# Last stores dealt over three queues, six pieces for the first batch's last chunk, and 140 half-size sets instead of 141

## The chip, the cores and the metric

The kernel runs on one core of one Trainium2 chip. The metric is the time of one execution in microseconds on the device; lower is better. The engines are named as in the profile: PE (TensorE, matrix products), ACT (ScalarE), DVE (VectorE), POOL (GpSimd) and SP (SyncE, which here only starts DMAs). DMAs are started from SP and ACT (hardware queues) and from POOL (a software queue).

## The reference

Inputs: `q`, `k`, `v` of shape 4 x 6080 x 256 (fp32), a scalar `tau` = 1, `w_in` of 256 x 2048 and `w_out` of 2048 x 256. Output: 24320 x 256 fp32.

```python
qn = q / (np.linalg.norm(q, axis=1, keepdims=True) + 1e-06)     # norm over the 6080 tokens
kn = k / (np.linalg.norm(k, axis=1, keepdims=True) + 1e-06)
s = kn.transpose(0, 2, 1) @ qn / tau                            # 256 x 256 for each batch
a = softmax(s)                                                  # over the last axis
x = (v @ a).reshape(24320, 256)
h = x @ w_in
g = 0.5 * h * (1 + tanh(sqrt(2 / pi) * (h + 0.044715 * h**3)))
out = g @ w_out
```

## The kernel before, in words

**Opening.** For batch 0 the 256 x 256 matrix kᵀq ("gram") and the sums of squares of q and k over the tokens ("ss") must be complete before anything else can start. q and k come in chunks of token rows (128 tokens to a row of the tile), cast to bf16 by POOL's DMAs. The last chunk, eight rows each of q and k, comes in pieces, `PIECES` (L137): (which, first row, end row), with which = 0 for q and 1 for k. DVE and ACT square the rows (`square_rows`), PE does the gram rows (`gram_first`, L210) and the sums (`ss_rows`, L229 and L235). Then come the scores, the softmax, and `aw` = a @ w_in, the attention matrix folded into the first weights, so that the rest is an MLP on v.

**Main part.** The 24320 tokens are cut into 25 blocks, numbered m = 0 to 24, each of two halves of up to 512 tokens. Batches 0 to 2 have six blocks each (5 x 1024 tokens and 960), batch 3 has seven (5 x 1024, 704 and 256). So block 22 has 1024 tokens, 23 has 704 and 24 (`LAST`) has 256. The hidden width 2048 is 16 chunks of 128, numbered 0 to f in hexadecimal. The first product of a block is done in one of two ways:

- plainly: a token `m:jct` is chunk c on half t (2 matmuls, L586; t = 2 means both halves at once), `m:Jct` its gelu on ACT (L598);
- as a half-size set, `m:sp...`, for the pair of chunks 2p and 2p+1 on both halves: seven half-size products m1 to m7 on sums of weights (`sw`, tokens `b:w..`, DVE) and sums of v (`tv`, tokens `m:vs..`, DVE) in place of eight, with two copies on ACT (`cq`, L669, and `y5`, L672), two additions on DVE (`ap`, L674, and `ax`, L677) and four gelus on ACT (`G0`, `G1`, `Gr`, `Gx`).

The second product of a block is seven products `M1` to `M7`, each in two parts A and B (L765), of sums `T..` and `x1` made by DVE, and is put together by `y5`, `y6`, `ap`, `ax`, `a12`. `c11`, `c12`, `c21`, `c22` turn the result (L794, DVE) into output layout, and `m:O0` and `m:O1` store the two halves, each by `store` (L808) in four DMAs, bi = 0 to 3. In block 22 one such DMA has 128 KB, in block 23 88 KB, in block 24 32 KB.

**What sets the order.** `ORDER` (L990) is one long table of tokens, written out by hand or by a planner; the program issues the work in exactly this order, and each engine does its part of it in this order. Other tokens are loads (`lq`, `lk`, `lv` on POOL; `lt`, the transposed copy of v, on SP), the work on the next batch's gram, and `b0:aw..`/`b0:ac..` (the later parts of `aw`: product and scaling). PSUM is eight banks: each product takes the bank that came free longest ago (`take`), and gives it back (`give`) when its reader is done. So a change of order also changes which product waits for which reader.

**Semaphores of the DMAs.** The DMAs of SP and ACT share eight completion semaphores, dealt in turn, and POOL's DMAs have another eight. A DMA is issued only after the last DMA with the same semaphore has landed. At the end (L1320) SP waits for all sixteen, in the order of their numbers.

Of the kernel before, what the change touches and what calls it, by code (L numbers as in the profile page):

```python
# [18 lines left out]
def kernel(  # L19
# [777 lines left out]
    def store(m, tj):  # L797
        b, t0, hc = SB[m]
        r0 = b * N + t0 + tj * hc
        dst = out[r0 : r0 + hc, :].rearrange("(x t) (b c) -> b t x c", t=32, b=4)  # L800
        ot = OT.pop((m, tj))
        for bi in range(4):
            eng = nc.sync
            if m == LAST:
# [3 lines left out]
            eng.dma_start(out=dst[bi], in_=ot[bi * 32 : bi * 32 + 32, 0 : hc // 32].rearrange("p x h c -> p x (h c)"))  # L808
# [187 lines left out]
0:j51 0:J21 0:jb1 0:s7m6 0:ja1 0:Jb1 0:s6ap 0:J51 0:J91 :pF0 0:Ja1 1:j00 0:s7ap :pS3 b0:w02 1:lt1
1:J00 0:s6m3 0:s7m3 0:s6m7 1:j50 0:s6ax 1:J50 0:j01 0:s7G1 b1:r0.0 :pS1 :pF1 0:jb0 0:j61 0:j11
0:s6G1 b1:r0.1 1:j10 0:Jb0 b1:lq1 0:s7m7 b1:lk1 b1:lq2 0:s6Gx 0:s7ax 0:s6m4 0:M1A 0:J01 1:j30 4:lv0
0:s7m4 0:J11 b1:r0.2 0:M1B b1:lq3 :pA12 0:T3a 0:s6Gr 0:s7Gx 1:J10 b1:lk3 :pS2 b1:lk2 b1:r0.3 0:x1
1:j31 1:j21 0:s7Gr 0:J61 1:vs0 0:M2A 3:lv0 1:j41 1:J30 1:J31 1:s3m1 1:j01 0:T1a 1:J21 2:lv1 0:M2B  # L1000
0:T2a 1:J41 0:T3b 1:s3cq 1:j11 b1:dk0 b1:lk4 1:J01 0:c11 b1:r1.0 b0:w03 b1:r1.1 b1:zk1 1:s3m2 0:T1b
1:J11 0:M5A b1:r1.2 0:M6A 1:s3m5 1:s4m1 1:s4m5 1:vs1 1:s3G0 b1:r1.3 0:T2b b1:zq0 1:s3m6 1:s3y5 0:M5B
1:s4cq 1:s4y5 1:s4m6 8:lv0 b1:lq4 1:s4m2 0:y5 1:s3ap 1:s4ap :pS4 0:M6B 1:s4G0 1:s4m3 0:ap 1:s3m7
1:j51 1:s3ax 1:s3m3 :pNA b1:r2.0 1:s4m7 b1:zq1 1:vs2 b1:r2.1 b1:lq5 1:J51 b1:f1.1 1:s3Gx 0:M7A
1:s3G1 1:s5m1 1:s3m4 1:s4G1 1:s5cq 1:s3Gr b1:r2.2 1:s4ax 0:T4a 0:M3A b1:lk5 1:s5m5 1:s5y5 b1:r2.3
1:s5m2 2:lv0 b1:f0.1 1:s4Gx 1:s5m6 0:M3B 1:s5ap 1:s5G0 1:s4m4 b1:zq2 1:s6m1 b1:r3.0 1:s6m5 1:s5m7
1:s5m3 0:M7B 0:c12 1:s6cq b1:f1.2 1:s5ax 1:s6m6 1:s6y5 1:s5m4 1:s6m2 1:s5G1 b1:r3.1 1:s5Gr b1:r3.2
2:lt0 1:s4Gr 1:j20 0:T4b 1:s6ap 0:ax 1:j40 1:s6m3 b1:dk2 1:s5Gx 1:s6G0 b1:r3.3 0:c22 1:T3a 1:s7m1
1:s6m7 1:J20 1:s7cq 0:M4A 1:s7m5 1:J40 1:s6ax 0:M4B 1:s7y5 1:s7m6 b1:r4.0 0:c21 1:s6G1 1:s7ap b1:zk3
1:s6Gx b1:zq3 1:M1A 1:T1a 1:M1B 1:s7m7 b1:r4.1 1:s7m3 0:O1 b1:r4.2 1:s6m4 1:x1 1:s7G1 2:lt1 1:s7ax  # L1010
2:j20 1:s7m4 1:s7Gx 1:s7Gr 1:T2a 1:s7m2 1:s6Gr 2:j10 1:s7G0 1:M2A 2:s2m1 1:T3b 2:j30 b1:f3.1 1:T1b
1:M6A 2:J10 2:vs0 1:M2B 2:J20 b1:zq5 b1:lq6 1:c11 b1:lk6 2:s2cq 2:vs1 1:M5A 2:s2m5 b1:zk5 2:s2m2
1:T2b 2:j11 2:s2y5 b1:lq7 2:s2m6 1:M5B 2:s2G0 2:s2ap 2:j01 1:T4a 2:s2m3 2:J11 2:J30 1:y5 2:s3m1
1:M6B 3:lv1 b1:f1.3 2:s2G1 2:s3cq 2:s2m7 1:ap b1:f2.1 2:J01 2:vs2 2:s3m5 2:s3m2 2:s3y5 2:s3m6 2:s2ax
2:s4m1 1:M3A 1:M3B 2:s3G0 b1:zq4 2:s4cq 2:s3ap 1:c12 b1:r4.3 2:s2Gx 2:s2m4 2:s3m3 2:s4m2 2:s4m6
1:T4b 2:s3m7 2:s2Gr 2:s3ax 2:s4G0 2:s4m5 2:s4y5 2:s3G1 2:j21 1:M7A 3:lt0 0:O0 b1:r5.0 2:J21 2:s4ap
2:s5m5 2:s3m4 2:s4m7 2:s5m1 b1:dk4 1:M7B 2:s3Gx 2:s6m5 2:s4m3 b1:r5.1 2:s3Gr 2:s5y5 b1:f3.2 2:s4ax
2:s5cq 2:s6y5 1:ax 2:s4m4 2:s4G1 1:c22 2:s5m6 2:s5ap 1:M4A 2:s5m2 2:j31 2:s4Gx 2:s5m7 1:O1 b1:f3.3
b1:f5.1 2:s4Gr 2:s6m1 2:s5m3 2:s5ax 3:lt1 2:s5G0 2:J31 2:s6cq 1:M4B 2:s5m4 b1:r5.2 2:s6m6 2:s7m1
b1:r5.3 b1:f3.4 1:c21 2:s5Gx 2:s5G1 b1:r6.0 2:s7m5 2:s5Gr 2:s7cq 2:s6m2 2:s6ap 2:s6m3 2:s6m7 2:s7m6  # L1020
2:s7m2 2:s7y5 2:s6G0 2:T3a 2:j00 2:s6G1 2:s7ap 3:j00 2:s6ax b1:lk7 b1:r6.1 b1:f4.1 b1:lq8 b1:zq6
3:j30 2:J00 2:s6Gx b1:dk6 2:s7G0 b1:r6.2 b1:r6.3 b1:lk8 2:s7m7 2:T1a 2:s7m3 2:M1A 2:s7G1 2:s7ax
b1:f5.2 2:s6m4 2:M1B b1:lk9 3:j31 2:s7m4 3:j11 3:J30 2:T2a 2:s6Gr 2:s7Gx 4:lv1 3:J31 b1:f6.1 b1:lq11
2:s7Gr 3:j20 3:vs0 2:M5A 3:s2m1 b1:lq9 2:T3b 3:J11 2:x1 3:J00 3:j21 b1:zq7 3:vs1 2:M2A 3:j01 3:J20
2:M2B b1:f5.3 2:T1b 3:J21 2:c11 3:s2cq 5:lv1 b1:r7.0 b1:zk7 3:s2m5 3:s2y5 2:T2b b1:r7.1 2:M6A 3:J01
b1:r7.2 3:s2m2 3:s2m6 3:s2ap b1:r7.3 5:lv0 3:vs2 3:s3m1 2:M5B b1:lk10 b1:zq8 3:s2G0 3:s2m3 3:s2m7
2:M6B 3:s3cq 2:y5 b1:f5.4 b1:lq10 3:s3m5 3:s3m6 3:s2ax b1:f7.1 2:ap b1:r8.0 3:s2G1 3:s3m2 3:s3y5
3:s2m4 3:j10 3:s2Gx b1:lk11 3:s3G0 2:M3A b1:f7.2 3:s4m1 b1:dk8 3:J10 b1:r8.1 3:s2Gr 3:s3ap b1:f8.1
2:M3B 3:s4cq 3:s3m7 3:s4m5 b1:f7.3 3:s3m3 3:s4m2 3:s4m6 2:c12 b1:zk9 3:s4y5 3:s5m1 2:M7A b1:r8.2
3:s4G0 3:s3G1 3:s5m5 3:s3ax 3:s4ap 3:s3Gx 3:s5cq 3:s4m7 b1:r8.3 3:s3m4 3:s4m3 b1:r9.0 3:s5y5 2:T4a  # L1030
b1:r9.1 4:lt1 3:s4ax 3:s3Gr 3:s5m6 3:s5m2 b1:r9.2 2:T4b 3:s4G1 3:s5G0 2:M7B 3:s5ap 2:ax b1:r9.3
3:s4Gx b1:zq9 3:s6m5 3:s5m7 3:s6m1 b1:r10.0 b1:f7.4 b1:r10.1 3:s6cq 2:M4A 4:lt0 3:s5ax 3:s5m3 3:s4m4
3:s6y5 b1:r10.2 3:s5Gx 3:s5G1 3:s4Gr 3:s6m6 3:s5m4 3:s6m2 b1:r10.3 b1:f9.1 3:s6G0 b1:dk10 3:s6ap
3:T3a b1:r11.0 3:s7m1 3:s5Gr 3:s7m5 3:s6m7 3:s6ax 3:s7cq b1:f9.2 3:s6m3 2:M4B 3:s7m6 3:s7m2 3:s7y5
3:s6G1 5:lt0 3:s6Gx b1:r11.1 3:s6m4 4:j21 1:O0 b1:r11.2 3:s7G0 3:s7ap 4:J21 2:c21 3:s7m7 3:s7ax
3:s7m3 4:j01 4:j11 3:s7m4 3:s6Gr 3:s7G1 3:T1a b1:r11.3 4:j00 4:s2m1 4:s3m1 3:s7Gx 4:vs0 3:T3b 2:O0
b1:gc 5:lt1 3:s7Gr 4:J11 3:M1A 3:M1B 4:s3cq 4:J00 3:M5A 4:vs1 4:s3m2 3:T1b 4:s2cq 4:s2m2 4:J01 3:x1
4:s3m6 4:s2m5 4:s3G0 3:T2a 3:M5B 4:vs2 4:s2m6 4:s3m5 4:s2y5 b1:zq10 3:M6A 3:T2b 4:s3y5 3:y5 7:lv0
3:M6B 3:M2A 4:s2ap 4:s2G0 4:s3ap 4:s2m7 b1:zq11 b1:f9.3 4:j31 3:ap 4:s3m3 b2:lq0 b1:zk11 4:s2ax
4:s3G1 3:M2B b1:f9.4 3:T4b 4:J31 b1:f11.1 4:s2m4 4:s2Gx 4:s3m7 4:s3ax b2:lk0 4:s2m3 4:s2Gr 4:j20  # L1040
b1:f10.1 8:lv1 4:s2G1 4:s4m5 3:M3A 4:s4m1 4:J20 6:lv0 4:s4cq 3:M3B 4:s4y5 3:c11 4:s3m4 4:s3Gr b2:lk2
6:lv1 4:s4m2 4:s4G0 4:j30 4:s5m5 4:s4m6 3:c12 b1:f11.2 4:s5m1 4:s3Gx b2:lq2 3:M7A 4:s4ap 4:s4m3
4:s5cq 2:c22 4:J30 4:s4G1 4:s4m7 4:s6m1 4:s5m6 4:s5y5 4:s5m2 3:M7B b1:f11.3 4:s6cq 4:s4ax 4:s4m4
b1:f11.4 b1:ss 4:s5ap 4:s5G0 3:T4a 4:s5m3 4:s6m5 4:s4Gx 4:s4Gr 4:s5m7 4:s5G1 4:s6m6 b1:sv 5:j11
b1:pow 4:s6m2 4:s6y5 4:j10 4:s5ax 4:s5m4 5:j21 5:J11 3:ax 4:s6ap 3:c22 4:s7m1 b1:kf 6:lt1 3:M4A
4:s5Gx 4:s5Gr 4:J10 4:s6m3 2:O1 4:s6m7 4:s7m5 5:J21 3:M4B b1:kr 4:s6G0 4:s7cq 4:s6G1 b1:krp 4:M1A
4:T3a 3:O1 5:j41 4:s7m6 4:s7y5 4:s6ax b1:S0 b1:S1 4:s7m2 3:c21 4:s7ap 4:M1B 4:s7m7 5:j50 4:T1a
b1:th1 5:j31 4:s6Gx 4:s6m4 b1:th0 4:s7G0 5:J41 b1:dn 4:x1 5:j30 4:s7m3 4:s7ax 4:s7m4 4:s6Gr 5:J31
4:s7G1 6:lt0 4:M2A 5:j51 4:s7Gr 5:J50 5:j01 5:j20 5:J30 4:T2a b1:rc0 5:j10 5:J01 5:vs0 5:j40 5:J51
# [275 lines left out]
```

## Time and profile before

| | us |
|---|---|
| time before, median of 3 runs | 682.67 (682.46 to 682.88) |
| the profiled execution's own time | 682.53 |
| its span, first to last instruction | 680.7 |
| PE busy | 659.0 |
| ACT busy | 639.9 |
| DVE busy | 631.3 |
| POOL busy | 89.4 |
| mean granted TensorE clock | 0.998 |

The profile is of one execution. Times in its views are counted from the span's start. A matmul's row gives its duration from entering to leaving, and consecutive matmuls overlap; the spacing of their starts is what they cost. A row of the chain of waits gives a start, a length, and the work that held the end of the kernel back in that time. In brackets behind a row of the timeline stands the idle time of the engine before it, and what ended it. A row of a DMA's issuing gives the time that the queue spent on starting it; its flight ("to landing") comes after.

### The profile page before, as it was taken

The page shows a single profiled execution, that of the slowest core. Times are in us where ns is not written, and L with a number is a line of the kernel's source. Part 1 is how long each engine was busy: PE and PEld are TensorE (multiplying, and loading weights), DVE is VectorE, ACT ScalarE, POOL GpSimd, SP SyncE. Part 2 cuts the span into 40 slices and gives each one's busy share as a digit, 9 for nine tenths or more (in the row PEclk, how much of TensorE's full clock was granted, in tenths as well). Part 3 has the DMA queues.
Part 4 walks back from the last instruction along what each step waited for, and adds up shares of the span by engine and source line. Part 5 has one row for each costly group of instructions (what it writes and reads, how often), then busy time and mean ns, then how long its engine had stood idle before and what let it go on. Part 6 is the DMA issues. An engine that isn't in the chain of part 4 may idle for free.

```text
span 680.7 us, 10235 instructions
## 1 busy us (share of the span) xinstructions
PE 659.0 (97%) x3415; PEld 332.1 (49%) x3475; DVE 631.3 (93%) x934; ACT 639.9 (94%) x1241; POOL 89.4 (13%) x163
## 2 busy tenths in 40 slices
...
GB/s 242 208 256 140 133 106 172 116 122 169 90 109 88 132 180 110 103 107 107 139 140 78 88 128 137 86 142 136 49 79 63 63 86 117 47 92 36 69 44 121
DMA packets 164773, 78.80 MB, mean 116 GB/s; under 512 B 148608, under 2 KB 153152, under 8 KB 164000
## 3 DMA queue, kind: packets, MB, share of 16 engines
...
## 4 chain that ended last, share of the span: by engine, by line
PE 88%; DMA 4%; ACT 4%; DVE 1%; issue 1%; POOL 0%; SPq 0%; DVEq 0%; ACTq 0%; POOLq 0%
PE u L765 23%; PE rb L654 17%; PE j L586 12%; PE p L765 11%; PE qb L654 8%; PE c L765 5%; PE G L308 4%; DMA qk<-in_k_dram 4%; PE qa L654 4%; PE awp L527 2%; ACT g L598 1%; ACT qa L669 1%; ACT g L682 0%; ACT yw L672 0%; ACT sq L278 0%
## 5 line engine op out<-in xcount | busy, mean ns | idle before, releaser
L765 PEld LDWEIGHTS <-wcomb 128*128 128x128 bf16 x1400 | 134.7, 98 | 145.4 <-issue 0.7
L765 PE MATMUL u<-t,wcomb 128*128 128x512 bf16 (+3 forms) x588 | 144.2, 368 | 0.5
L598 ACT ACTIVATE g<-j 128x512 bf16<-128x512 f32 (+2 forms) x204 | 123.2, 657 | 1.6 <-PE j L586 1.5
L586 PE MATMUL j<-vT,aw 128*128 128x512 bf16 (+3 forms) x425 | 114.8, 367 | 0.7 <-DVE aw L419 0.3
L674 DVE TENSOR_TENSOR qb<-rb,yw 128x512 f32<-128x512 f32 (+2 forms) x141 | 95.9, 682 | 7.2 <-ACT yw L672 3.0
L677 DVE TENSOR_TENSOR xw<-rb,yw 128x512 f32<-128x512 f32 (+2 forms) x141 | 94.6, 672 | 6.7 <-PE rb L654 4.5
L654 PE MATMUL rb<-tv,sw 128*128 128x512 bf16 (+2 forms) x275 | 100.3, 374 | 0.4
L765 PE MATMUL p<-g,wcomb 128*128 128x512 bf16 (+3 forms) x385 | 95.3, 368 | 0.8
L688 ACT ACTIVATE g<-xw 128x512 bf16<-128x512 f32 (+2 forms) x141 | 94.5, 673 | 0.4 <-DVE xw L677 0.3
L672 ACT ACTIVATE yw<-qb 128x512 f32<-128x512 f32 (+2 forms) x141 | 89.2, 639 | 1.4 <-PE qb L654 0.9
L669 ACT ACTIVATE qa<-rb 128x512 f32<-128x512 f32 (+2 forms) x141 | 89.8, 641 | 0.8 <-PE rb L654 0.2
L682 ACT ACTIVATE g<-qb 128x512 bf16<-128x512 f32 (+2 forms) x141 | 88.2, 636 | 1.9 <-PE qb L654 1.7
L685 ACT ACTIVATE g<-rb 128x512 bf16<-128x512 f32 (+2 forms) x141 | 88.5, 639 | 0.3
L679 ACT ACTIVATE g<-qa 128x512 bf16<-128x512 f32 (+2 forms) x141 | 88.6, 637 | 0.2
L654 PEld LDWEIGHTS <-sw 128*128 128x128 bf16 x564 | 55.2, 98 | 58.0 <-DVE ot L794 0.4
L586 PEld LDWEIGHTS <-aw 128*128 128x128 bf16 x440 | 42.7, 98 | 43.3 <-issue 1.7
L654 PEld LDWEIGHTS <-aw 128*128 128x128 bf16 x423 | 41.4, 98 | 42.5 <-DVE aw L540 0.2
L746 DVE TENSOR_TENSOR t<-g,g 128x2048 bf16<-128x2048 bf16 (+3 forms) x50 | 58.2, 1164 | 0.9 <-ACT g L595 0.4
L738 DVE TENSOR_TENSOR g<-g 128x2048 bf16<-128x2048 bf16 (+3 forms) x50 | 58.2, 1163 | 0.2
L744 DVE TENSOR_TENSOR t<-g,g 128x2048 bf16<-128x2048 bf16 (+3 forms) x50 | 58.1, 1162 | 0.2
L748 DVE TENSOR_TENSOR t<-t,g 128x2048 bf16<-128x2048 bf16 (+3 forms) x50 | 57.6, 1157 | 0.0
L321 POOL DMA_DIRECT2D vb<-in_v_dram x47 | 24.1, 514 | 240.4 <-PE rb L654 103.3
...
## 6 DMA issues: line engine op xcount, KB each, us to landing
...
wst<-in_moe_w_out_dram POOLq DMA_DIRECT2D x2, 1024.0 KB, 11.3
...
```

The lines of the kernel that those rows point to most:

```text
L586: GATE[0] = nc.tensor.matmul(hp[:, :n].rearrange("p (t x) -> p t x", t=2) if t == 2 else hp[:, :n], lhsT=AW[b][:, cc, fc * 128 : fc * 128 ...
L598: nc.scalar.activation(g[:, t, fc % 8, :hc], hp[:, :hc], AF.Gelu_apprx_tanh)
L654: GATE[0] = nc.tensor.matmul(acc[:, :hc], lhsT=lhs, rhs=rhs, start=i in (1, 5), stop=True, skip_group_check=True)
L669: nc.scalar.activation(Q0[m, p][:, :hc], RB[m, p][:, :hc], AF.Copy)
L672: nc.scalar.activation(YW[m, p][:, :hc], Q1[m, p][:, :hc], AF.Copy)
L674: nc.vector.tensor_add(Q1[m, p][:, :hc], RB[m, p][:, :hc], YW[m, p][:, :hc])
L677: nc.vector.tensor_add(XW[m, p][:, :hc], RB[m, p][:, :hc], YW.pop((m, p))[:, :hc])
L679: nc.scalar.activation(g[:, 0, e, :hc], Q0.pop((m, p))[:, :hc], AF.Gelu_apprx_tanh)
L682: nc.scalar.activation(g[:, 1, e, :hc], Q1.pop((m, p))[:, :hc], AF.Gelu_apprx_tanh)
L685: nc.scalar.activation(g[:, 0, e + 1, :hc], RB.pop((m, p))[:, :hc], AF.Gelu_apprx_tanh)
L688: nc.scalar.activation(g[:, 1, e + 1, :hc], XW.pop((m, p))[:, :hc], AF.Gelu_apprx_tanh)
L765: GATE[0] = nc.tensor.matmul(ACCS[m, acc][:, :hc], lhsT=wcomb[:, w, fc, :], rhs=x[:, fc, :], start=first and k_ == 0, stop=k_ == 3, skip_g ...
```

## The change

There are three parts.

1. The last chunk of batch 0 comes in six pieces in place of five: q rows 0-3, k rows 0-2, k 3-4, k 5-7, q 4-6, q 7. The squares, gram rows and sums that follow are cut and ordered to match.
2. The four stores of 23:O0 go to SP, POOL, ACT and SP; all four of 23:O1 go to POOL; the last two of 22:O0 and 22:O1 go to POOL. (Before: of block 23 the first two of each half to SP, the last two to POOL; of block 22 all to SP.) Those of block 24 stay with ACT and SP by turns.
3. The table has 4054 tokens in place of 4061. The set 0:s6 (15 tokens) is taken out, and its chunks c and d of block 0 are done plainly (8 tokens: jc0, jc1, jd0, jd1 and their gelus). The tokens of blocks 0 to 3 ahead of 3:s6m1 and those after 23:s4ax stand in another order; from 3:s6m1 to 23:s4ax the two tables are the same.

```diff
-    PIECES = [(0, 0, 4), (1, 0, 5), (1, 5, 8), (0, 4, 6), (0, 6, 8)]
+    PIECES = [(0, 0, 4), (1, 0, 3), (1, 3, 5), (1, 5, 8), (0, 4, 7), (0, 7, 8)]
...
             if m == LAST:
                 eng = (nc.scalar, nc.sync)[bi % 2]
-            elif m == LAST - 1 and bi > 1:
+            elif m == LAST - 1 and tj == 0:
+                eng = (nc.sync, nc.gpsimd, nc.scalar, nc.sync)[bi]
+            elif m == LAST - 1 or m == LAST - 2 and bi > 1:
                 eng = nc.gpsimd
...
-        for i in range(4):
+        for i in range(3):
             gram_first(c, i)
         ss_rows(c, 0, range(0, 4))
+        gram_first(c, 3)
         ss_rows(c, 1, (0, 1, 4))
         square_rows(c, 1, 5, 8, "dve")
-        square_rows(c, 0, 4, 6, "dve")
+        square_rows(c, 0, 4, 7, "dve")
         ss_rows(c, 1, range(5, 8))
-        for i in (4, 5):
+        for i in (4, 5, 6):
             gram_first(c, i)
-        ss_rows(c, 0, range(4, 6))
-        square_rows(c, 0, 6, 8, "dve")
-        for i in (6, 7):
-            gram_first(c, i)
-        ss_rows(c, 0, range(6, 8))
+        ss_rows(c, 0, range(4, 7))
+        square_rows(c, 0, 7, 8, "dve")
+        gram_first(c, 7)
+        ss_rows(c, 0, range(7, 8))
...
 ORDER = """                       # the first tokens
-0:j00 0:J00 0:j10 0:j20 b0:aw2 0:J20 b0:aw3 0:j30 b0:aw5 b0:aw4 b1:lq0 0:J30 b0:ac2 0:J10 b0:ac3
-b0:aw6 b0:aw7 b0:ac5 0:j60 b0:ac4 b0:ac6 b0:w00 b0:w01 0:j50 0:J60 0:j70 0:s6m1 1:lv1 0:J70 0:vp1
...
+0:j00 0:j10 b0:aw3 b0:aw2 0:j20 b0:ac2 b0:ac3 0:j30 0:J30 b0:aw5 b0:ac5 b0:aw4 b0:ac4 b0:aw7 b0:aw6
+0:J20 0:j50 0:J00 b0:w00 b0:ac7 0:J10 b0:ac6 0:j60 0:vp1 0:j40 b1:lq2 0:vc10 0:j90 0:vc11 0:J50 0:jc0
+0:s7m1 b1:lq0 0:J60 0:J40 1:lv1 0:vs0 b1:lk0 0:J90 0:Jc0 0:jd0 0:vs1 0:ja0 0:j01 0:Jd0 0:jb0 0:s7cq
...
                                # the last tokens
-23:c21 24:T4b 24:y5 23:M2B 24:y6 24:M3A 24:M7A 24:T4a 24:M7B 23:c11
-24:ax 24:M3B 24:a12 24:M2A 23:O1 24:M2B 24:c22 24:M4A 23:O0 24:c12 24:M4B 24:c21 24:O1 24:c11 24:O0
+24:y5 24:M6B 24:T4a 24:y6 23:O1 23:M2B 24:M3A 23:c21 24:M7A 24:M7B 24:T4b 24:M3B 23:c11
+23:O0 24:M2A 24:ax 24:M2B 24:a12 24:M4A 24:c22 24:c12 24:c11 24:M4B 24:c21 24:O1 24:O0
```

More of the change, by code (lines that the diff above doesn't have):

```diff
@@ L996 @@
[L996 to L1049, printed above, removed]
@@ L1056 @@
-5:s6cq 4:M7A 5:s5m7 5:s4Gx b2:dk0 5:s6m5 5:s4m4 5:s6m6 5:s6y5 5:s5ax 5:s6m2 5:s5m3 4:M7B 5:s4Gr
-5:s6ap 6:j40 5:s5m4 b1:w02 4:ax 5:s6G0 5:s5G1 5:s6m7 b1:w10 5:s5Gx 5:s7m1 5:s7m5 4:M4A 5:s5Gr 5:s6ax
-7:lt0 5:s7cq 5:s7y5 5:s7m6 4:c22 5:s6m3 b1:w01 5:s7ap 4:M4B 4:c21 6:j50 6:J40 5:s7m2 5:s6Gx 5:s6m4
-5:s7m7 b2:zk1 6:j01 6:j21 5:s7G0 5:s7m3 b1:w12 b1:w03 6:s3m1 5:s7ax 5:T3a 5:s6Gr 6:J50 5:s7m4 4:O0
-6:J01 5:M1A 5:M1B 3:O0 7:lt1 5:s7Gr 6:vs0 6:s3cq 5:s6G1 6:j10 6:j11 5:s7G1 5:x1 6:s3m2 b1:w11 6:vs1
@@ L1124 @@
-11:s2y5 11:s2G0 10:M5B 11:s3y5 11:s2ap 11:s3m1 11:J00 11:s2m7 11:s2m3 b2:w00 11:s2ax 10:M6A 11:s2m4
-11:s3cq 11:s2G1 11:s3m6 10:y5 11:s2Gr 11:s3m2 10:T4a 11:s3G0 11:s3ap 11:s4m1 10:M6B 11:j20 16:lv0
-11:s4m5 b2:w01 11:s3m3 11:s4cq 16:lv1 11:s3m7 11:s2Gx 10:ap 11:s4m2 10:M3A b2:w10 11:J20 11:s3ax
-11:s3m4 11:s4y5 11:s3G1 11:s4m6 11:s4ap 14:lv1 10:M7A b3:lq0 11:s3Gx 11:s3Gr 11:s5m5 11:s4G0 11:s5m1
-11:s4m7 11:s5y5 11:s6m1 11:s5cq 10:T4b b3:lk3 11:s4m3 10:M3B 11:s4ax 11:s4m4 b2:w12 11:s5m6 b3:lq3
@@ L1204 @@
-16:M5A 17:s2G1 b3:w02 17:s3cq 15:O0 17:s3y5 17:s2m7 b3:aw7 17:s3m6 17:s3m2 17:s2G0 b3:ac7 17:s2ax
-b3:w00 17:s3G0 16:M5B 16:y5 17:s3ap 16:T4a 17:s5m1 17:s4m1 17:s4cq 17:s2m4 16:M6B 17:s3m3 17:s4m6
-b3:w10 16:ap 17:s3m7 17:s2Gr 17:s3G1 17:s2Gx 17:s4m2 17:j00 17:s4m5 b3:w11 17:s4G0 16:M7A 17:s4y5
-17:s5cq 17:s3ax 16:M7B 17:s5m6 17:J00 17:s3m4 17:s4ap 15:O1 17:s5m5 17:s4m7 17:s3Gx b3:w01 16:ax
-19:lv1 17:s4m3 16:M3A 17:s5y5 17:s4ax 17:s5ap 17:s3Gr 17:s5m2 17:s4G1 b3:w03 17:s6m1 19:lt1 17:s4m4
-17:s4Gx 17:s5m7 17:s5ax 17:s6cq 16:T4b 17:s5m3 16:M3B 17:s5G1 17:s4Gr 17:s6m6 17:s5Gx 17:s5m4
@@ new lines @@
+0:M1B 0:T3a b1:r0.0 0:J51 0:x1 0:j71 b1:r0.1 b1:lk2 0:s7G1 b1:lq1 0:s7Gr 0:J71 b1:lk1 b1:r0.2 0:Jc1
+8:lv0 1:s3m1 b1:r0.3 1:j31 1:j20 :pS2 0:M2A 1:J30 :pS1 3:lv0 0:M2B 1:vs0 1:J31 1:s3cq 1:s3m2 1:J20
+0:s7Gx 1:j11 1:s3G0 0:T1a b1:lk5 0:T2a 1:vs1 1:j51 2:lv1 1:j41 0:T3b 1:J11 1:s3m6 0:c11 1:j21 0:M6A
+b1:lk3 0:T1b :pNA 1:J51 1:j01 1:s3m5 b1:zq0 1:J41 0:M5A 0:M5B b1:lq4 1:J01 1:j00 b0:w03 1:s3y5 0:T2b
+1:s4m1 1:s3ap 1:J21 b1:r1.0 1:s4m5 0:y5 b1:r1.1 :pS4 b1:r1.2 1:vs2 1:J00 1:s3m7 0:M6B 1:s3ax 1:s3m3
@@ new lines @@
+5:s6m7 b1:w10 5:s5Gx 5:s7m1 5:s7m5 4:M4A 5:s5Gr 5:s6ax 7:lt0 5:s7cq 5:s7y5 5:s7m6 4:c22 5:s6m3
+b1:w01 5:s7ap 4:M4B 4:c21 6:j50 6:J40 5:s7m2 5:s6Gx 5:s6m4 5:s7m7 b2:zk1 6:j01 6:j21 5:s7G0 5:s7m3
+b1:w12 b1:w03 6:s3m1 5:s7ax 5:T3a 5:s6Gr 6:J50 5:s7m4 4:O0 6:J01 5:M1A 5:M1B 3:O0 7:lt1 5:s7Gr 6:vs0
+6:s3cq 5:s6G1 6:j10 6:j11 5:s7G1 5:x1 6:s3m2 b1:w11 6:vs1 6:j41 5:s7Gx 6:J10 5:T1a 5:M2A 6:s3m5
+5:M2B 6:s3m6 5:T3b 6:J11 b2:zq1 6:vs2 5:T1b 6:s3y5 6:J21 6:s3ap 5:T2a 5:M5A 6:J41 5:M5B 6:s3G0 6:j20
+6:s3m3 6:j30 b1:w13 b2:zq0 5:T2b 6:s3m7 6:s4m1 8:lt1 6:s3ax 5:M6A 5:y5 6:J20 5:M6B 6:J30 6:s3m4
@@ new lines @@
+7:s7y5 b2:r5.0 8:J01 7:s6ax 7:s7m2 b2:lk8 7:s6G1 b2:r5.1 b2:f4.1 7:s5m4 13:lv1 7:s7G0 7:s7m6 7:s6Gx
+8:j10 8:J10 7:s6m4 8:j20 7:s7ap b2:r5.2 7:s5Gr 7:s7m7 8:J20 7:T3a 8:j11 9:lv1 7:s7ax 8:J11 7:s7Gx
+7:T1a 7:s7m3 7:M1A 7:s7m4 8:s2m1 b2:r5.3 8:vs0 7:s7G1 7:s7Gr 8:s2cq 7:s6Gr 8:vs1 8:j00 b2:r6.0 7:M1B
+7:T3b 8:s2m5 7:T2a 8:j30 8:s2m6 8:s2y5 8:J00 8:s2m2 8:s2ap 8:J30 b2:r6.1 8:j21 b2:r6.2 7:M5A 8:s2m3
+8:vs2 b2:r6.3 7:T1b 7:x1 8:s2G0 8:s2m7 8:s3m1 8:s2ax 8:s2G1 7:M2A 7:M2B 8:s2m4 8:J21 7:T2b b2:zk7
@@ new lines @@
+b2:r11.2 9:s5ap b2:f9.4 8:ax 9:s4G1 10:J20 b2:r11.3 9:s5m3 9:s7m1 9:s4Gr 9:s5m7 9:s6m5 9:s4Gx 9:j00
+b2:f10.1 b2:gc 8:M4A 9:s5G1 9:s6cq 9:s6y5 9:J00 10:lt1 9:s5ax 9:s6m6 b2:f11.2 9:s7cq 9:s6m2 b2:f11.3
+9:s6ap 9:s5m4 8:M4B 9:s7m5 9:s6m7 9:s5Gr 9:s5Gx 9:s7m6 9:s7m2 9:j30 b2:f11.4 9:s7y5 8:c21 9:s7G0
+9:s6ax 9:s6G0 9:s6m3 10:j30 b2:ss 9:s7ap 9:s6m4 10:j10 7:O1 8:c22 9:J30 13:lt1 9:s7m7 10:s2m1 b2:sv
+9:T3a 9:s6Gx 9:s7m3 9:s7ax 9:T1a 10:s3m1 9:s6Gr 9:M1A 9:s7m4 10:J30 10:vs0 9:s6G1 10:s2cq 9:s7G1
```

501 lines of the change are left out of this document (276 added, 225 removed).

## The prediction

> **What bounds the kernel now.** The page first: which engine is full, and what the chain of work that ended last is made of.
>
> ```profile
> PE 659.0 (97%) x3415; PEld 332.1 (49%) x3475; DVE 631.3 (93%) x934; ACT 639.9 (94%) x1241; POOL 89.4 (13%) x163
> PE 88%; DMA 4%; ACT 4%; DVE 1%; issue 1%; POOL 0%; SPq 0%; DVEq 0%; ACTq 0%; POOLq 0%
> ```
>
> Matmuls make the time: 88% of the chain. An average hides the stages, so the table by stretches comes next (per engine busy us and instruction count; then clock, DMA share, GB/s).
>
> ```profile
> 37.30:60.00 22.70, 22.07 (x115) 10.68 (x117) 20.09 (x38) 21.13 (x42) 4.74 (x8) 1.00 0.84 191
> 60.00:100.00 40.00, 39.79 (x198) 19.56 (x201) 39.41 (x54) 40.00 (x73) 7.40 (x15) 1.00 0.82 143
> 674.40:680.70 6.30, 0.00 (x0) 0.00 (x0) 0.52 (x2) 0.00 (x0) 0.31 (x1) 0.82 0.48 92
> ```
>
> From 60 to 100 us PE is busy 39.79 of 40, and ACT 40.00: both full, so ACT too can set the pace there. In the first 23 us after the opening both have holes. The last 6.30 us hold no matmul at all: only stores. So three places can move: the opening (before 37.3), the holes up to 60 us, and the 6.3 us of stores. The order table is unchanged from token 3:s6m1 to 23:s4ax; I take the middle as rigid and only carry a shift through it. The profiled execution took 682.53 us, 680.7 of it span and 1.83 around it; it lies 0.14 under the median 682.67, so I add my sum to the median. About 0.2% of this, 1.37 us, is what a measurement of this kernel can tell from no change.
>
> **Part 1, six pieces.** The chain of waits at the end of the opening (start, us, what):
>
> ```profile
> 31.42 1.03 PE G L210 x8
> 32.63 0.87 PE ss L235 x6
> 34.48 0.09 PE ss L229 x4
> 34.59 0.27 ACT lnq L378
> ```
>
> After the k piece that lands at 31.4, the chain holds matmuls without a gap: it is PE's backlog, not data. The last data, a two-row q piece, is squared on DVE at:
>
> ```profile
> 33.68 0.43 DVE L182 TENSOR_TENSOR sq<-qk 128x512 bf16<-128x512 bf16 x1 [0.28 <-DMA qk<-in_q_dram]
> DMA packets 2032, 1.82 MB, mean 202 GB/s; under 512 B 140, under 2 KB 1778, under 8 KB 2032
> ```
>
> The second row is the DMA view of 27 to 36 us. One row of the chunk is 128x256 bf16, 65.5 KB; at 202 GB/s it takes 0.32 us. So the three-row piece q4-6 lands about one row before the end of the data, 33.66-0.32 = 33.34, and the last row near 33.7. DVE squares three rows in at most 0.56 (a 768-wide square at 31.40 took that), 33.34 to 33.9, and the last one by 34.2. PE meanwhile has six matmuls of rows 4 to 6 to do (0.11 each, from 1.03 for eight less the overhang) and reaches the last sum near 34.4, as before. What hides the sixth piece is this backlog; without it, the piece's own fixed cost (0.1 at most; I have no row for it) shows. Term: +0.05, between -0.1 and +0.2. All later GpSimd loads move by one semaphore; the first of them, a weight load of the 1.2 MB that follow, is wanted only after 35 us: no cost.
>
> **Part 2, one half-size set fewer, blocks 0 to 3 in a new order.** The set's 7 matmuls become 8: one 512-wide one more. ACT's 6 operations become 4, DVE's 2 go. Prices by start-to-start spacing, since row durations overlap:
>
> ```profile
> 49.62 1.46 PE L586 MATMUL j<-vT,aw 128*128 128x512 bf16 x6
> 43.61 0.59 PE L586 MATMUL j<-vT,aw 128*128 128x512 bf16 x2
> 44.56 0.38 PE L654 MATMUL qa<-vT,aw 128*128 128x512 bf16 x1 [0.35 <-DVE sw L620]
> 50.92 0.38 PE L654 MATMUL rb<-tv,sw 128*128 128x512 bf16 x1
> 51.43 1.08 PE L586 MATMUL j<-vT,aw 128*128 128x512 bf16 x4
> 37.33 1.28 ACT L421 ACT_TABLE_LOAD   x1
> 38.62 1.09 ACT L598 ACTIVATE g<-j 128x512 bf16<-128x512 f32 x2
> 42.07 0.60 ACT L598 ACTIVATE g<-j 128x512 bf16<-128x512 f32 x1 [1.07 <-PE j L586]
> ```
>
> Six in 1.46 with the last 0.38 long: (1.46-0.38)/5 = 0.216 a matmul. Two ACT operations span 1.09, one 0.60: 0.49 each. So PE pays +0.216 and ACT is relieved of 2 x 0.49 = 0.98.
>
> The holes: the second of the two at 43.61 starts at 43.83; the next matmul should follow 0.216 later, at 44.04, and starts at 44.56: 0.52 lost to the weight sums on DVE (L620). From 50.92 to 51.43 is 0.51, so 0.30 lost. Four matmuls in 1.08 against 3 x 0.216 + 0.38 = 1.03: 0.05. These three are 0.87 of what PE loses before 60 us; smaller stalls, each near the last one, bring my walk of the trace to 1.1 (an estimate).
>
> The new order puts the set's matmuls behind more plain ones, so its weight sums (tokens b0:w10, w01, w11) have longer to be ready; walking it by the spacings above, with PSUM's eight banks taken and given in the table's order, I find two stalls left, about 0.25 (1:s3m1 wants the bank of 0:s7G1) and 0.08: 0.33. The price of this order: ACT's first gelu is now J30, the fourth chunk, after eight matmuls of j and four of aw: 37.34 + 12 x 0.216 + 0.16 of overhang = 40.1 rather than 38.62. ACT starts 1.5 later but then finds four chunks ready; before, it idled 1.07 at 41.0 and in smaller pieces around it, and it has 0.98 less to do. So ACT should reach 60 us no later than before. Its cover is those holes of before; if they reappear, its 40.00 of 40.00 carries any lateness on. Net for PE: +0.22 - (1.1-0.33) = -0.55; bounds -0.85 (no stall left) and +0.2 (all as before).
>
> One load is moved on a queue that matters: block 1's second v load now issues behind two q loads on GpSimd, not one.
>
> ```profile
> 43.41 0.53 POOL L321 DMA_DIRECT2D vb<-in_v_dram  x1 [2.68 <-PE rb L654]
> DMA to landing us min/median/max: 7.5/7.5/7.5
> L333 SPq DMA_TRANSPOSE vT<-vb x1: 1335/1335/1335, 52.5 to 52.5; - x1
> DMA to landing us min/median/max: 3.1/3.1/3.1
> 59.27 1.08 PE L586 MATMUL j<-vT,aw 128*128 128x512 bf16 x4
> ```
>
> Before, it landed at 50.9, its transposed copy issued at 52.5 and landed at 55.6, and the first matmul on it ran at 59.27. One 256 KB load more ahead of it is 1.3 us at 202 GB/s: 52.2, still before the copy's old time. The 3.6 us to its use cover it.
>
> **Part 3, the stores.** Here a wait does go. All HW stores (SP and ACT) share eight completion semaphores dealt in a ring; a store first waits until the ring's previous user has landed. GpSimd has eight of its own.
>
> ```profile
> 674.35 4.17 SPq L808 DMA_DIRECT2D out_dram<-ot  x4
> 674.36 2.09 ACTq L808 DMA_DIRECT2D out_dram<-ot  x4
> DMA to landing us min/median/max: 3.3/3.3/3.3
> 674.65 0.28 DVE L794 STREAM_TRANSPOSE ot<-c 128x128 f32<-128x128 f32 x1
> SPq L808 <- DMA out_dram<-ot: 2.5, 1, 2.5
> L808 SPq DMA_DIRECT2D out_dram<-ot x2: 315/369/423, 677.7 to 678.1; - x2
> DMA to landing us min/median/max: 1.5/1.5/1.6
> L1320 SPq EVENT_SEMAPHORE  x4: 17/28/28, 678.6 to 678.8; - x4
> ```
>
> The data is ready at 674.93 (the transpose at 674.65), yet SP's last two stores issue at 677.7 and 678.1: 2.5 us on a DMA, ACT's store of the same block's other half (issued 674.36; the 3.3 is its flight, so it landed near 677.7). They land 1.5 and 1.6 after, the last at 679.7; from there to the span's end is 1.0.
>
> After, by the rings of the two compiled programs, the last four stores find block 23's 88 KB stores ahead of them: SP's first waits for ACT's, ACT's second and SP's second for SP's two. By the neighbours:
>
> ```profile
> L808 SPq DMA_DIRECT2D out_dram<-ot x2: 316/390/465, 673.2 to 673.6; - x2
> DMA to landing us min/median/max: 1.9/2.1/2.4
> 675.30:676.50 1.20, 0.00 (x0) 0.00 (x0) 0.00 (x0) 0.00 (x0) 0.00 (x0) 1.00 0.98 200
> 677.70:678.50 0.80, 0.00 (x0) 0.00 (x0) 0.00 (x0) 0.00 (x0) 0.00 (x0) 0.92 0.00 0
> L808 POOL DMA_DIRECT2D out_dram<-ot x4: 627/642/688, 667.8 to 674.1; - x4
> out_dram<-ot SPq DMA_DIRECT2D x4, 32.0 KB, 1.9
> out_dram<-ot ACTq DMA_DIRECT2D x4, 32.0 KB, 2.9
> ```
>
> ACT's stores fly 1.0 longer than SP's (2.9 against 1.9). SP's 88 KB ones take up to 2.4, so ACT's, issued near 673.4, lands 673.4 + 2.4 + 1.0 = 676.8 at worst, 675.9 at best (1.9 in place of 2.4, issued 673.3 less what the queue saves); I take 676.3. Then SP issues at 676.3 and 676.7 instead of 677.7 and 678.1, 1.4 sooner. But the DMA engines are 0.98 busy until the queue empties near 677.9, so the flight is not 1.5 but towards 1.9: landing 678.6, between 678.3 and 679.3, against 679.7: -1.1.
>
> Given back: SP ends by waiting for each semaphore in number order, (678.8-678.6)/3 = 0.07 apart. Before, the last store was on number 6 of 0 to 7, one wait before the end; after, it is on number 1, with six behind: five more x 0.07 = +0.35. GpSimd's five stores take at most 0.69 each to write, and four of them belong to 23:O1, which stands ahead of 23:O0 in the table: off the path. PE's tail is reordered with the same matmuls; I walk +0.05 there. Sum of part 3: -1.1 + 0.35 + 0.05 = -0.7; bounds -1.1 (six waits free) and 0 (flights stretch until the queue is as late as it was).
>
> A rule that speaks against this part: the Trainium skill, "DMA: Bandwidth & Descriptors", section "Issuing engines are not separate DMA queues", says that DMAs from scalar, sync and gpsimd run on the same 16 engines, and that starting them on several saves only the time to start them. The 0.98 at 675.3 agrees; the 0.00 from 677.7 to 678.5 does not: there the engines stand idle while a store waits for a semaphore. By the rule part 3 would be worth nothing, as SP starts as many stores as before.
>
> Sum: +0.05 - 0.55 - 0.7 = -1.2; 682.67 - 1.2 = **681.5 us**.
>
> **The rivals.**
>
> More of both (0.24): the tail gives its -1.1, the order its -0.85: 682.67 + 0.05 - 1.95 = 680.8. For it: 0.8 us of DMA standing idle just where the stores move to. Against it: the six waits behind the last store.
>
> The stores are bound by the DMA engines (0.17): they issue sooner and fly longer, landing as late as before, part 3 at 0: 682.67 + 0.05 - 0.55 = 682.2. For it: 0.98 busy. Against: the idle 0.8.
>
> ACT keeps the pace (0.17): PE's removed stalls come back between 60 and 100 us as waits for banks that ACT frees, so only the extra matmul counts: 682.67 + 0.05 + 0.22 - 0.7 = 682.2. For it: 40.00 of 40.00. Against: ACT is relieved of 0.98.
>
> Slower: the late first gelu (0.08). Place: ACT's queue, 38.6 to 60 us. It starts 1.5 late and has 0.98 less to do; each us it then idles beyond what it idled before (22.70-21.13 = 1.57) is a us for PE, through the banks. Price: at 4 us idle 1.5 - 0.98 + 2.4 = +2.9, so 682.67 + 0.05 + 2.9 - 0.7 = 684.9. It makes the kernel slower from 1.8 us of idle after 40.1, and by 0.2% from 3.1. Against it: four chunks stand ready when ACT starts.
>
> **How the numbers follow.** The forecast, all three terms near their values, has 0.34, with a range of its own of 681.0 to 682.0; the others as given. Eight in ten lie from 680.6 (both terms at their best, the opening 0.1 better) to 682.8. Faster means under 681.30: all of the first rival and half of the forecast's lower side, 0.43; slower means over 684.04: 0.07; the rest, 0.50, is within 0.2%.
>
> **What would show it.** Right: SP's wait on a DMA at the store line falls from 2.5 to about 1, its last stores issue before 677, and the idle DMA stretch is gone; the last landing at 678.6 with six semaphore waits after it; the stretch 37.3 to 60 us shows PE's wait for the weight sums gone; ACT's first gelu near 40.1 without a hole after it; the tokens from 3:s6m1 run some 0.5 earlier than before. Wrong: the last landing at 679.4 or later, new PE waits for ACT between 60 and 100 us, or last opening sums later than 34.6.

## The result, and the profile after

The change makes the kernel slower: 683.55 us (median of 22 runs, 683.11 to 684.41) against 682.66 (22 runs), a ratio of 1.0014 with a 95% interval of 1.0008 to 1.0021. That is +0.9 us where -1.2 was forecast, and above the range of eight in ten, which ended at 682.8. It is less than the 0.2% that the prediction took for the least a measurement can tell, but the interval lies clear of 1. The profiled execution has a span of 681.8 us.

First the page, its engines and its chain of work that ended last:

```profile
PE 659.2 (97%) x3416; PEld 332.2 (49%) x3476; DVE 629.8 (92%) x932; ACT 638.7 (94%) x1239; POOL 92.4 (14%) x169
PE 89%; DMA 5%; ACT 3%; issue 1%; DVE 1%; POOL 0%; SPq 0%; ACTq 0%; DVEq 0%; POOLq 0%
```

PE has 0.2 us more work, ACT and DVE have less, as the removed set says. The table by stretches of the kernel after:

```profile
37.30:60.00 22.70, 22.18 (x117) 10.81 (x119) 19.85 (x38) 20.76 (x41) 3.88 (x8) 1.00 0.92 190
60.00:100.00 40.00, 39.79 (x198) 19.62 (x201) 39.08 (x54) 39.97 (x73) 7.97 (x16) 1.00 0.81 144
674.40:678.20 3.80, 0.00 (x0) 0.00 (x0) 0.48 (x2) 0.00 (x0) 0.00 (x0) 1.00 0.60 117
```

PE and ACT are as full from 60 to 100 us as before, and from the start of the first j matmul to the start of PE's last matmul it took 636.35 us where it had been 636.81, so this is not where the time went. What is new is in the last row: from 674.4 to 678.2, when PE has nothing left, DVE still has two instructions to do. The timeline of that stretch (start, us, engine, line, operation; in brackets the idle time before and what ended it):

```profile
673.77 0.51 DVE L794 STREAM_TRANSPOSE ot<-c 128x128 f32<-128x128 f32 x2
674.30 4.75 SPq L810 DMA_DIRECT2D out_dram<-ot  x4
674.31 4.81 ACTq L810 DMA_DIRECT2D out_dram<-ot  x4
677.72 0.32 DVE L794 STREAM_TRANSPOSE ot<-c 128x128 f32<-128x128 f32 x1 [3.44 <-DMA out_dram<-ot]
677.96 0.27 DVE L794 STREAM_TRANSPOSE ot<-u 128x128 f32<-128x128 f32 x1
```

The two transposes of 24:O0, done by 674.93 before, start at 677.72: DVE sat idle for 3.44 us on a DMA that reads an output tile. The chain of waits at the end names the same:

```profile
674.31 0.37 ACTq L810
674.68 0.04 issue
674.72 2.71 DMA out_dram<-ot
```

That DMA is ACT's second store of 24:O1. A store should not hold back a transpose of another half, unless both use one buffer. The output tiles come from a pool of three buffers (`yout`, tag `ot`), and which tile gets which is settled when the program is compiled. The addresses in the two compiled programs:

```
tile        before    after
ot22_1      214464    214464
ot23_1      222656    222656
ot23_0      218560    218560
ot24_1      214464    214464
ot24_0      222656    214464
```

Before, 24:O0's tile takes the buffer of 23:O1, whose stores have landed by 673.4. After, it takes that of 24:O1, the half stored just ahead of it. So the last four stores issue at 678.3 to 678.7, land by 680.4, and eight semaphore waits follow (the last to land is on number 0, so its own wait and seven more):

```profile
L1322 SPq EVENT_SEMAPHORE  x8: 28/28/28, 680.4 to 680.9; - x8
SPq L810 <- DMA out_dram<-ot: 0.5, 1, 0.5
```

The second row, of SP's waits, shows that the change did what was wanted of it: SP's wait on a DMA at the store line fell from 2.5 us to 0.5. The wait came back on DVE, larger.

### The profile page after: what moved, and what is told of

Same layout as the page of the kernel before. It is cut to its first block, busy times and chain, and to the rows that moved or that the text cites. A ratio compares the mean times of both kernels' runs of the same rounds, so it can differ in the third digit from the quotient of the medians.

```text
span 681.8 us, 10222 instructions
## 1 busy us (share of the span) xinstructions
PE 659.2 (97%) x3416; PEld 332.2 (49%) x3476; DVE 629.8 (92%) x932; ACT 638.7 (94%) x1239; POOL 92.4 (14%) x169
## 4 chain that ended last, share of the span: by engine, by line
PE 89%; DMA 5%; ACT 3%; issue 1%; DVE 1%; POOL 0%; SPq 0%; ACTq 0%; DVEq 0%; POOLq 0%
PE u L765 23%; PE rb L654 17%; PE j L586 13%; PE p L765 11%; PE qb L654 8%; PE c L765 5%; PE G L308 4%; PE qa L654 4%; DMA qk<-in_k_dram 2%; PE awp L527 2%; DMA qk<-in_q_dram 2%; DMA out_dram<-ot 1%; ACT g L682 1%; ACT qa L669 0%; ACT sq L278 0%
## 5 line engine op out<-in xcount | busy, mean ns | idle before, releaser
L688 ACT ACTIVATE g<-xw 128x512 bf16<-128x512 f32 (+2 forms) x140 | 92.0, 659 | 0.1
L669 ACT ACTIVATE qa<-rb 128x512 f32<-128x512 f32 (+2 forms) x140 | 87.4, 628 | 0.8 <-PE rb L654 0.2
L672 ACT ACTIVATE yw<-qb 128x512 f32<-128x512 f32 (+2 forms) x140 | 86.8, 626 | 1.5 <-PE qb L654 1.0
L682 ACT ACTIVATE g<-qb 128x512 bf16<-128x512 f32 (+2 forms) x140 | 86.2, 623 | 1.6 <-PE qb L654 1.4
L685 ACT ACTIVATE g<-rb 128x512 bf16<-128x512 f32 (+2 forms) x140 | 86.3, 625 | 0.6 <-PE rb L654 0.3
L679 ACT ACTIVATE g<-qa 128x512 bf16<-128x512 f32 (+2 forms) x140 | 86.2, 624 | 0.2
```

The source lines that it names most:

```text
L669: nc.scalar.activation(Q0[m, p][:, :hc], RB[m, p][:, :hc], AF.Copy)
L672: nc.scalar.activation(YW[m, p][:, :hc], Q1[m, p][:, :hc], AF.Copy)
L679: nc.scalar.activation(g[:, 0, e, :hc], Q0.pop((m, p))[:, :hc], AF.Gelu_apprx_tanh)
L682: nc.scalar.activation(g[:, 1, e, :hc], Q1.pop((m, p))[:, :hc], AF.Gelu_apprx_tanh)
L685: nc.scalar.activation(g[:, 0, e + 1, :hc], RB.pop((m, p))[:, :hc], AF.Gelu_apprx_tanh)
L688: nc.scalar.activation(g[:, 1, e + 1, :hc], XW.pop((m, p))[:, :hc], AF.Gelu_apprx_tanh)
```

## The experiments

Times of one table come from runs beside the kernel before on the same chip; the kernel before was at 682.42, 682.40 and 682.44 us in the three groups (e1 to e4, e5 to e8, e9 to e11).

| kernel | us | ratio to before (95%) |
|---|---|---|
| e1_slot | 681.10 | 0.9982 (0.9973 to 0.9991) |
| e2_tail | 683.55 | 1.0017 (1.0008 to 1.0026) |
| e3_order | 682.02 | 0.9994 (0.9986 to 1.0003) |
| e4_pieces | 682.52 | 1.0001 (0.9992 to 1.0010) |
| e5_dealing | 684.05 | 1.0024 (1.0014 to 1.0034) |
| e6_tailorder | 682.53 | 1.0002 (0.9993 to 1.0011) |
| e7_best | 680.90 | 0.9978 (0.9969 to 0.9987) |
| e8_last7 | 681.05 | 0.9981 (0.9972 to 0.9990) |
| e9_shared | 684.17 | 1.0025 (1.0016 to 1.0034) |
| e10_nopool | 681.13 | 0.9980 (0.9971 to 0.9989) |
| e11_poollast | 682.30 | 0.9998 (0.9989 to 1.0007) |

**e1_slot: the changed kernel, with a buffer apart for 24:O0.**

```diff
-            OT[m, tj] = yout.tile([128, 16, 2, 32], FP32, tag="ot", ...)
+            if (m, tj) == (LAST, 0):
+                OT[m, tj] = lastp.tile([128, 4, 2, 32], FP32, tag="otl", ...)
+            else:
+                OT[m, tj] = yout.tile([128, 16, 2, 32], FP32, tag="ot", ...)
```

> The changed kernel, with one edit: the output tile of 24:O0 gets a buffer of its own instead of one of the pool's three. Theory A (the loss sits in a shared buffer: 24:O0's tile was given the buffer of 24:O1's, so its two transposes wait 3.4 us until 24:O1's stores have landed): the transposes end near 674.9, SP's last two stores issue near 676.3 and 676.7, the last landing near 678.6; with the opening 0.42 later and the blocks 0.46 earlier as the profile of after shows, 682.66 + 0.42 - 0.46 - 0.7 = 681.9 us. Rival (the DMA engines bound the end whatever the buffer): last landing at 680 or later, 683.2 or more.

681.10 us, 1.3 under the kernel before and 2.2 under the changed one, each against the kernel before beside it. Theory A holds, and the rival falls. The timeline of its end:

```profile
674.22 0.27 DVE L798 STREAM_TRANSPOSE otl<-c 128x128 f32<-128x128 f32 x1
674.41 0.28 DVE L798 STREAM_TRANSPOSE otl<-u 128x128 f32<-128x128 f32 x1
676.04 0.87 SPq L814 DMA_DIRECT2D out_dram<-otl  x2
```

The transposes end at 674.7 and SP's last two stores issue at 676.0 and 676.5; the last landing is at 678.1. The time is 0.8 under what was expected of theory A: the tail gave 1.1 rather than 0.7, and the opening's 0.42 of the profile after was not there (its chain ends at 34.59, as in the kernel before).

**e2_tail, e5_dealing, e6_tailorder: which part of the tail does it.** e2 has the new dealing and the new order of the last tokens on the kernel before, e5 the new dealing alone, e6 the new order alone.

```diff
 # e5: store() of the change, table of before
-            elif m == LAST - 1 and bi > 1:
+            elif m == LAST - 1 and tj == 0:
+                eng = (nc.sync, nc.gpsimd, nc.scalar, nc.sync)[bi]
+            elif m == LAST - 1 or m == LAST - 2 and bi > 1:
                 eng = nc.gpsimd
 # e6: store() of before, the table's tokens after 23:s4ax from the change; e2: both
```

> The kernel before, with only the new dealing of the stores and the new order of the last tokens. Theory A: the buffer is shared here too, the transposes wait 3.4 us, the last stores land 0.7 later and the semaphore waits behind them add 0.35 or so: 682.66 + 1.1 = 683.8 us. Rival (the loss comes from the opening or the new first blocks): 682.0 us.

> The kernel before, with only the new dealing of the stores; all tokens in the old order. In the compiled program 24:O0's tile again has the buffer of 24:O1's. Theory A (dealing decides the buffer, and the buffer the loss): the last transposes wait until 24:O1's stores land, near 677.5, and the time is that of the dealing with the new tail order, 1.1 over the kernel before: 683.5 us. Rival (it takes the new order of the last tokens): 682.4 us or less.

> The kernel before, with only the new order of the last tokens; the stores are dealt as before. The compiled program gives 24:O0's tile a buffer apart from 24:O1's. Theory A: the transposes end near 674.9, SP's last stores again wait for ACT's, 682.4 us within 0.2. Rival (the order of the tail is what makes the transposes late): 683.5 us.

683.55, 684.05 and 682.53 us: the dealing is enough, the order alone is worth nothing that can be told. In e2 and e5 the two tiles of block 24 have the same address, in e6 they have not. e5 is 0.55 over what was expected. Its last store lands as in e2 (680.6 and 680.5), but SP's last two drains, behind all stores, start 0.34 us apart in its trace and 0.05 apart in e2's; why is not shown. DVE's waits in e5's last stretch:

```profile
DVE ot L794 <- DMA out_dram<-ot: 3.5, 1, 3.5
```

and SP's in e6, whose stores wait for ACT's as in the kernel before:

```profile
SPq L808 <- DMA out_dram<-ot: 2.6, 1, 2.6
```

Why the pool picks that buffer under the new dealing stays open. With SP for the first two stores of 23:O1 in the changed kernel, the compiled program has the tiles apart again. So it seems to hang on all four of 23:O1's stores being GpSimd's.

**e9_shared: the shared buffer alone.** The kernel before, and both tiles of block 24 from a pool with one buffer.

```diff
+            if m == LAST:
+                OT[m, tj] = lastp.tile([128, 4, 2, 32], FP32, tag="otl", ...)   # bufs=1
```

> The kernel before, with the output tiles of 24:O1 and 24:O0 put into one buffer on purpose; dealing, order and opening as before. Theory A: this alone makes 24:O0's transposes wait until 24:O1's stores have landed (677.9 in the kernel before), so the last stores issue near 678.4 and land near 680.5: 1.0 more, 683.4 us. Rival (the shared buffer needs the new dealing to hurt): 682.4 us.

684.17 us: the direction of theory A, but 1.7 in place of 1.0. The wait is longer than I took it:

```profile
678.67 0.32 DVE L798 STREAM_TRANSPOSE otl<-u 128x128 f32<-128x128 f32 x1 [4.50 <-DMA out_dram<-otl]
```

In this program the semaphores fell otherwise, too: SP's stores of 24:O1 waited for ACT's of the same half, and landed at 678.55 instead of 677.7. So a shared buffer needs no new dealing to hurt; its price depends on how the stores ahead of it are queued.

**e3_order: the first blocks alone.** The table's tokens ahead of 3:s6m1 from the change, the rest as before.

> The kernel before, with only the new order of blocks 0 to 3 and the set 0:s6 done plainly. Theory B (the order gives what the traces show between the first j matmul and 200 us): 682.66 - 0.46 = 682.2 us, PE's wait for the weight sums near 44 us gone. Rival (ACT keeps the pace, only the extra matmul counts): 682.9 us.

682.02 us, 0.4 under the kernel before; the interval reaches from -0.95 to +0.2, so by times alone it is not told from no change. The trace speaks for theory B: its list of waits names none of PE between 37.3 and 100 us, and in the table by stretches

```profile
37.30:60.00 22.70, 22.46 (x118) 10.65 (x119) 20.11 (x35) 20.59 (x40) 4.24 (x8) 1.00 0.90 191
```

PE is busy 22.46 of the 22.70 us against 22.07 before (0.04 of the difference is the wait for the first weights, which this execution had behind it at 36.9).

**e4_pieces: the six pieces alone.** `PIECES` and the opening's squares, gram rows and sums from the change.

> The kernel before, with only the last chunk's load in six pieces and the opening's squares, gram rows and sums to match. Theory C (the sixth piece itself costs, through later landings of the k pieces and ACT's square of k rows 3 to 4): first j matmul near 37.75, 682.66 + 0.4 = 683.1 us. Rival (the landings of that one execution were late by chance): 682.7 us.

682.52 us, +0.1 with an interval from -0.5 to +0.7: nearer the rival. Its opening's chain ends where that of the kernel before did, 34.59:

```profile
31.38 0.64 ACT sq L180
32.52 0.96 PE ss L235 x6
34.65 0.27 ACT lnq L378
```

The sixth piece cost the loads nothing here: the last two pieces land at 33.33 and 33.66, and the last of five had landed at 33.66 too. From 32.52 on the chain is PE without a gap, but it leads back through a square on ACT (L180) to the landing of k rows 3 and 4 at 31.36. In the profile after, this landing is at 31.74.

Over the profiles the same step lay between 34.15 and 34.87 in nine executions with five pieces (and 34.59 in the kernel before), and at 34.59, 34.65 and 35.02 in three with six. So the 0.42 of the profile after is mostly that execution's; 0.1 or 0.2 may be the pieces'.

**e7_best: the better version.** The changed kernel, a buffer apart for 24:O0, the opening in five pieces.

> The changed kernel with a buffer of its own for 24:O0, and the opening as before in five pieces. Theory C (the six pieces are worth nothing that can be measured): as with six pieces, 1.3 under the kernel before, 681.1 us. Rival (they cost 0.1 to 0.4): 680.7 to 681.0 us.

680.90 us, the fastest here: 1.5 under the kernel before. Whether six pieces cost 0.2 can't be told, as the intervals of e1 and e7 overlap.

**e8_last7, e10_nopool, e11_poollast: what ends the kernel then.** e8 moves two stores of block 21 to GpSimd, so that the last store is on the last semaphore that SP waits for. e10 takes 23:O0's store off GpSimd as well; e11 is e7 with a store of 24:O0 on it.

```diff
 # e8
-            elif m == LAST - 1 or m == LAST - 2 and bi > 1:
+            elif m == LAST - 1 or m == LAST - 2 and bi > 1 or m == LAST - 3 and tj == 0 and bi > 1:
 # e10: e8, and
-                eng = (nc.sync, nc.gpsimd, nc.scalar, nc.sync)[bi]
+                eng = (nc.sync, nc.scalar, nc.scalar, nc.sync)[bi]        # and 21:O1's bi = 3 on GpSimd
 # e11: e7, and
-                eng = (nc.scalar, nc.sync)[bi % 2]
+                eng = nc.gpsimd if tj == 0 and bi == 0 else (nc.scalar, nc.sync)[bi % 2]
```

> As e7_best, with two more stores (21:O0, bi 2 and 3) on GpSimd, so that every later SP and ACT store takes the semaphore two numbers lower and the last one is on number 7 instead of 1. Theory D (the six waits in number order behind the last landing cost 0.06 each): 0.35 to 0.4 less than e7_best. Rival (the end is set by something beside these waits): the same as e7_best.

> As e8_last7, with no store of 23:O0 on GpSimd (SP, ACT, ACT, SP; a third store of block 21 goes to GpSimd instead, so that the last store is still on semaphore 7). Theory E (in e7_best and e8_last7 the end is set by GpSimd's own drain, which ends 4.7 us after its last store is written, and this ate the gain of the six waits): GpSimd is through by 675, the end follows the last landing by 1.0, and with 352 more small packets on the hardware queues the landing is up to 0.5 later than in e7_best: 680.4 to 680.9 us. Rival (the drain is only waiting with the others): the packets alone count, 681.2 to 681.5 us.

> As e7_best, with the first store of 24:O0 on GpSimd instead of ACT. Theory E: written near 675.0, GpSimd's drain ends near 679.7 and the end comes 0.75 later: 1.4 over e7_best, 682.3 us. Rival (a GpSimd store costs no more than its landing, some 3 us after issue like the others): 680.9 us.

e8: 681.05, nothing gained over e7. The waits behind the last landing are gone, as theory D has it (SP is through 0.08 after its last landing at 678.3), but the end didn't follow. GpSimd's own last drain (the instruction that ends its work) was through at 679.0, 0.5 after SP; in e7 it was through at 678.3, 0.1 after SP at 678.2. (All of e8's end is 0.6 later than e7's, because its matmuls are: their last starts at 674.30 against 673.68.) The drains of e7, e8 and e11 (ns, least, median and longest; first and last start):

```profile
L1315 POOLq DRAIN  x3: 46/93/5356, 673.0 to 678.8; - x3
```

```profile
L1315 POOLq DRAIN  x3: 46/102/5399, 673.6 to 679.5; - x3
```

```profile
L1315 POOLq DRAIN  x3: 46/93/4997, 674.6 to 680.1; - x3
L1315 SPq DRAIN  x3: 7/7/7, 678.4 to 679.8; - x3
674.59 0.57 POOL L814 DMA_DIRECT2D out_dram<-otl  x1 [0.93 <-DVE otl L798]
```

The last row is the timeline's, of the store that e11 moved to GpSimd. The long drain begins with GpSimd's last store and takes 5.0 to 5.4 us here: it ends 4.4 to 4.75 us after that store has been written, which took 0.6, and 2.2 to 2.3 us after it has landed (676.2 to 677.3). In e11 SP's first drain is at 678.4, and the long drain on GpSimd lasts until 679.6: 1.1 us in which all wait for GpSimd. 682.30 is what theory E expected. In e1, e7, e8 and e11 alike the span ends 0.77 to 0.79 us after this drain; in the kernel before, where SP is through last, 1.4 us after it. e10, with GpSimd out of it, is at 681.13, between the two theories: its end is SP's again, but its last landing is 0.8 later than e7's (678.5 against 677.65). Of this 0.15 is its later matmuls; the rest fits the one more 88 KB store that goes through the hardware queues, but no run shows that apart. So GpSimd's drain is last in e7 by only 0.1 us, and taking its last store away won nothing.

## Why the prediction was wrong

**The stores (forecast -0.7, measured +1.1).** The failed step is "The data is ready at 674.93 (the transpose at 674.65)". That holds for the kernel before; after, the second transpose starts at 677.96 and ends at 678.2. I took DVE's end from before and looked only at who waits for a semaphore on SP. Whether the transposes could run at that time was a matter of which buffer their tile has, and the new dealing changed that. It could have been read from the compiled program, where the first of the two waits for four semaphores of SP and ACT; I read the stores there, not the transposes. The working behind the step held: with the buffer apart (e1), SP's last stores issue at 676.0 and 676.5 (forecast 676.3 and 676.7), the last landing is at 678.1 (678.6), the six waits in number order are there, and from the start of PE's last matmul to the end it is 5.4 us against 6.5 before: -1.1 where -0.7 stood. Mis-sized was the landing, 1.6 sooner than before rather than 1.1: ACT's 88 KB store landed at 675.6 rather than 676.3, and the last store flew 1.7 us rather than 1.9. The semaphore waits beyond the last landing were right, but not alone: the end followed it 0.46 later than before (forecast 0.35), because GpSimd's drain ends at 678.8, 0.1 after SP is through. I put GpSimd's stores "off the path"; for 23:O0's that is not so.

**The rule.** By the Trainium skill, "DMA: Bandwidth & Descriptors", section "Issuing engines are not separate DMA queues", starting DMAs on several engines saves only the time to start them. From that the prediction made a part 3 worth nothing, "as SP starts as many stores as before"; SP starts six fewer (four of block 22, two of block 23). The measured effects are larger both ways: -1.1 us in the tail with the buffer apart, +1.1 with the buffer shared. What the starting engine decided here was which semaphore and which buffer is waited for. That the stores share the DMA engines is not contradicted: engines that stand idle behind a wait, the 0.00 of the prediction, say nothing about it.

**The first blocks (forecast -0.55; -0.4 in e3, which its times don't tell from nothing).** Right in mechanism where the traces show it. In the profile after, PE's wait for the weight sums is gone, one stall of 0.30 near 58 us is left where I had 0.25, and ACT started its gelus late without carrying it on:

```profile
37.76 1.28 ACT L421 ACT_TABLE_LOAD   x1
40.34 3.24 ACT L598 ACTIVATE g<-j 128x512 bf16<-128x512 f32 x6 [1.29 <-PE j L586]
```

Six gelus in a row follow, in place of the hole of 1.07 before. PE's stalls before 60 us add up to 0.42 (the 0.30 and the 0.12 below) where 0.33 was forecast, which with the 1.1 of before and the extra matmul's 0.22 gives -0.46: just the 636.35 us against 636.81. What I had called covered was nearly not: the transposed copy of block 1's v.

```profile
L333 SPq DMA_TRANSPOSE vT<-vb x1: 1342/1342/1342, 54.6 to 54.6; - x1
DMA to landing us min/median/max: 4.5/4.5/4.5
```

Its load landed at 52.45, near the 52.2 forecast, but a wait of SP for a matmul of PE held the copy until 54.6, which the prediction did not count. So it issued 2.1 us later than before, and it flew 4.5 in place of 3.1, landing at 59.1, just as its matmul was due: 0.12 us of PE lost. The 3.6 us of cover were used up. In e8 it flew 5.0, and PE waited for it:

```profile
PE j L587 <- DMA vT<-vb: 0.5, 1, 0.5
```

Kernels with the new order spread: from the first j to the start of PE's last matmul their seven profiles have 636.31 to 636.79, the six with the old order 636.75 to 636.93. The waits behind the slower ones differ. In e8 (636.70) and e11 (636.58) it is this copy, which flew 5.0 and 4.9 us; in e1 (636.79) it is a later transposed copy, for which PE waited 0.2 us before a matmul at 89.6. So the cover of the new order is thin, and in e1's profile it won nothing.

**The opening (forecast +0.05, measured +0.1, not told from nothing).** The landings came as forecast (33.33 in e4 for 33.34). PE's chain without a gap to the last sum fits the backlog, but what starts it with six pieces is ACT's square of k rows 3 and 4, which the prediction left out.

**The sum.** Alone, the parts give -0.40 + 0.10 + 1.13 = +0.83, and the whole +0.89: they add up. Without the shared buffer e1 has -1.3 where -1.2 stood, but that the numbers are so near is luck in part: the tail gave more than its term and the first blocks less, and in e1's profile the tail is all of the gain. Of the rivals none named the shared buffer. The slower one looked for its time in ACT's queue; the right place was a wait on DVE for a store. Two numbers of the prediction don't follow from their own words: the first rival and half of the forecast make at most 0.24 + 0.17 = 0.41 for faster, not 0.43, and the slower rival turns to a loss from 1.7 us of idle, not 1.8.
